# Where a pair's transposes, a batch part's values and the first FFN units stand: one reordering of an attention and gated-FFN kernel

## The chip, the cores and the metric

One NeuronCore of a Trainium2 chip. The metric is the device time of one execution in microseconds (us), the median of three runs. The kernel takes float32 inputs, computes in bfloat16 with float32 accumulation, and writes float32.

## The reference

```python
scores = q @ k.transpose(0, 1, 3, 2) / sqrt(64)      # 8 batches, 12 heads, 448 x 448
attn   = maximum(scores, 0) ** 2 / 448
x      = attn @ v                                    # heads side by side: 3584 tokens x 768
gate   = maximum(x @ w_gate, 0)                      # 768 -> 1536
out    = (gate * (x @ w_val)) @ w_out                # 1536 -> 768
```

There is no softmax: a score is cut at zero and squared. All constant factors are taken together into one scale, applied to the output.

## The kernel before, in words

The whole kernel is unrolled Python. Every instruction is pinned, so on each engine the instructions stand in the order in which the Python code emits them, and each engine works through its own list in that order. Waits come from semaphores alone.

Batches are counted from zero here. Batch 0 runs in `first_batch`, batches 1 to 7 in `batch(b)`. The FFN of batch b is cut into units (`ffn_units`) that are put between the attention work of batch b + 1, so that TensorE (PE) always has matmuls. There are two kinds of units.

- `gv_unit`: twelve matmuls of 448 columns into `g_ps`, ScalarE's relu into `g_sb`, twelve into `v_ps`, VectorE's product of both into `hT`. There are 12 such units for each batch. PE takes 2.27 us for one.
- `out_unit`: 24 matmuls of 384 columns into `o_ps`, ScalarE's scaled copy into `o_sb`, and, after the second of a tile's two units, two stores of 192 KB from SyncE's queue. There are 6 such units after an even batch, 8 after an odd one.

`mm2` issues each matmul as two halves of 64 output columns, which run side by side.

The attention of a batch works on six pairs of heads, `hp` 0 to 5, which make three parts, `qd` 0 to 2. A part has seven score tiles (`QUAD`: three for each of its two pairs and one `last` with the last 64 keys of both) and one values tile (`av`). `batch(b)` takes these 24 tiles in eight bursts of three. For each score tile, PE makes four matmuls on 64 x 64 quarters of its array, ScalarE does a relu from PSUM (`r_sb`, L166), VectorE squares it into `attn` (L170). The third tile of a burst is put into `late`, and its relu comes after the relu of the next FFN unit. For the values tile, `av_last` goes with the burst, and `av_rest` (12 matmuls) later; then VectorE copies the part's result into `xT` (L401).

A pair needs its k and q transposed. For batches 0 to 2, `transposes` does this on PE: 16 small transposes into `kq_ps` (L159), and a VectorE copy into `kq_sb` (L161). From batch 3 on (`PE_B`), DMA transposes do it, and `transpose_pair` emits nothing for PE. `PAIR_AT` says after which burst which pair's transposes come; the pair is used in the next burst or the one after it.

The score tiles, the values tiles of batches 1 to 7 and `kq_ps` share three PSUM buffers (tag `sc`) in turn; the FFN accumulators and the values banks of batch 0 share two (tag `acc`). A tile that takes a buffer waits until the tile before it in that buffer has been read.

How many units stand between two bursts is set by `gaps`: each burst n has `(before, after)` slots, before and after its `av_rest`. `gap()` takes the next share of the units that were there at the batch's start. Before, batch 1 has `[(1, 1), (1, 0)] * 4`, twelve slots, and the others sixteen. Batch 0's first six units run between batch 0 and batch 1, with the transposes of batch 1's pair 0 between the fifth and the sixth.

`low_values(b)` (L108) is a VectorE copy of some 64 rows of v within SBUF; it reads the first of the two pieces in which v is loaded. `batch(1)` does it at its start; for later batches `batch(b)` does it for b + 1 after burst 5, behind the values copy.

All loads go through GpSimd's DMA queue in program order: k, q and v of batch 0, the weights in pieces with k, q and v of batch 1 between them, `w_out` in two halves (kf 0 to 5 and 6 to 11), then k, q and v of batch 2, and so on.

In `first_batch` there are no FFN units yet; `idle_matmuls` on zeros keep PE at work. The values of part qd come with burst n as `av_at` says, and VectorE copies the two banks into `xT` (L369).

The functions that the diff touches, with the lines of the profile:

Of the kernel before, what the change touches and what calls it, by code (L numbers as in the profile page):

```python
# [11 lines left out]
AF = mybir.ActivationFunctionType  # L12
# [4 lines left out]
def kernel(  # L17
# [15 lines left out]
    nc = tc.nc  # L33
# [7 lines left out]
    NQ = HP // 2  # L41
    KD = d_model // 128
    KF = d_ff // 128
# [16 lines left out]
    def pin(ins):  # L60
        return tc.keep_in_program_order(ins)

    def mm(o, l, r, start, stop):
        pin(nc.tensor.matmul(o, lhsT=l, rhs=r, start=start, stop=stop, skip_group_check=True))  # L64

    def mm2(o, l, r, start, stop):

        for c in range(2):
            p = slice(c * 64, c * 64 + 64)
            mm(o[p], l[:, p], r, start, stop)  # L70
# [71 lines left out]
    def operands(b, hp):  # L142

        if b >= PE_B:
            n = b % NB
            return kT_b[n][:, hp, 0:S], qT_b[n][:, hp, 0:S]
        kq = transposes(b, hp)
        return kq[:, 0:S], kq[:, 512:512 + S]
# [15 lines left out]
    def relu_part(src, n):  # L164
        r = rpool.tile([128, 2, S], BF16, name="r_sb")[:, :n, :]
        pin(nc.scalar.activation(r, src, AF.Relu))  # L166
        return r
# [25 lines left out]
    def av_last(b, qd, attn, banks):  # L193

        for c, p in HALVES:
            for h2, o in HALVES:
                mm(banks[c][o, :], v_b[b % NB][p, 4 * qd + 2 * c + h2, 3, :], attn[p, 6 + h2, :], True, False)
# [7 lines left out]
    def av_bank():  # L205
        return psum.tile([128, 512], FP32, name="xT_ps", tag="acc", bufs=2)[:, :S]

    def idle_matmuls(ps, n):

        for _ in range(n):  # L210
            mm2(ps, blank[:, 0:128], blank, True, True)


    late, late_squares = [], []

    def flush_relu():
        while late:
            src, dst, n = late.pop(0)
            late_squares.append((dst, relu_part(src, n)))

    def flush():
        flush_relu()
        while late_squares:
            square_part(*late_squares.pop(0))

    def gv_unit(b, mf, xT, hT):
        c = max(i for i, (f0, _) in enumerate(CHUNKS) if f0 <= mf * 128)
        f = mf * 128 - CHUNKS[c][0]
        col = (b % 2) * S
        g_ps = psum.tile([128, 512], FP32, name="g_ps", tag="acc", bufs=2)[:, :S]  # L230
        for kd in range(KD):
            mm2(g_ps, wg_sb[c][:, kd, f:f + 128], xT[:, kd, :], kd == 0, kd == KD - 1)
        g_sb = gpool.tile([128, S], BF16, name="g_sb")
        pin(nc.scalar.activation(g_sb, g_ps, AF.Relu))  # L234
        flush_relu()
        v_ps = psum.tile([128, 512], FP32, name="v_ps", tag="acc", bufs=2)[:, :S]
        for kd in range(KD):
            mm2(v_ps, wv_sb[c][:, kd, f:f + 128], xT[:, kd, :], kd == 0, kd == KD - 1)
        pin(nc.vector.tensor_tensor(hT[:, mf, col:col + S], v_ps, g_sb, ALU.mult))  # L239
        flush()  # L240

    def segment_rows(b0, s):

        b, s = b0 + s // 7, s % 7
        r = out[b * S:(b + 1) * S, :]
        i, half = divmod(s, 2)
        if half:
            return r[256:448, :].rearrange("(j i) m -> i j m", i=3)[i]
        return r[0:256, :].rearrange("(j i) m -> i j m", i=4)[i]

    def out_unit(b0, t, c0, c1, hT, state):

        if c0 == 0:
            state[t] = opool.tile([128, d_model], FP32, name="o_sb")
        o_sb = state[t]
        o_ps = psum.tile([128, 512], FP32, name="o_ps", tag="acc", bufs=2)[:, :c1 - c0]
        for kf in range(KF):
            mm2(o_ps, hT[:, kf, bass.ts(t, 128)], wo_sb[kf // 6][:, kf % 6, c0:c1], kf == 0, kf == KF - 1)
        flush()
        pin(nc.scalar.activation(out=o_sb[:, c0:c1], in_=o_ps, func=AF.Copy, scale=float(out_scale)))  # L260
        pieces = b0 == B - 2 and t == 6
        if pieces or c1 == d_model:
            m = slice(c0 if pieces else 0, c1)
            for s in range(2):
                e = nc.sync
                if pieces and c0 > 0:
                    e = nc.gpsimd if c1 < d_model else (nc.sync, nc.scalar)[s]
                pin(e.dma_start(out=segment_rows(b0, 2 * t + s)[:, m], in_=o_sb[s * 64:s * 64 + 64, m]))  # L268

    hT_of, xT_of, o_state = {}, {}, {}  # L270
# [20 lines left out]
    def gap():  # L291

        n, of, i = share
        for _ in range((i + 1) * n // of - i * n // of):
            ffn.pop(0)()
        flush()
        share[2] = i + 1
# [22 lines left out]
    def transpose_pair(b, hp):  # L320
        kqs[b, hp] = operands(b, hp)
# [6 lines left out]
    def burst(b, tiles):  # L328

        todo, begun = [], None  # L330
        for qd, kind, c, i in tiles:
            attn = attn_of(b, qd)
            if kind == "pair":
                todo.append(scores(kqs[b, 2 * qd + c], i, attn, 8 * c + 2 * i))
            elif kind == "last":
                todo.append(scores_last((kqs[b, 2 * qd], kqs[b, 2 * qd + 1]), attn))
            else:
                ps = sc_tile()
                banks = [ps[:, c, :S] for c in range(2)]
                av_last(b, qd, attn, banks)  # L340
                begun = (qd, banks, ps[:, :, :S])
        return todo, begun

    def first_batch():
        banks = [av_bank(), av_bank()]
        idle_matmuls(banks[0], 14)
        transpose_pair(0, 0)
        idle_matmuls(banks[0], 4)
        av_at = {3: 0, 5: 1, 6: 2}
        for n in range(len(tiles_first) // 3):  # L350
            todo, _ = burst(0, tiles_first[3 * n:3 * n + 3])
            if n in av_at:
                av_last(0, av_at[n], attn_of(0, av_at[n]), banks)
            relu2(*todo[0])
            if n not in av_at:
                idle_matmuls(banks[0], 2)
            if n + 1 < HP:
                transpose_pair(0, n + 1)
            if n not in av_at:
                idle_matmuls(banks[0], 1)  # L360
            relu2(*todo[1])
            relu2(*todo[2])
            if n == 2:
                low_values(0)
            if n in av_at:
                qd = av_at[n]
                av_rest(0, qd, attn_of(0, qd), banks)
                for c in range(2):
                    pin(nc.vector.tensor_copy(xT_of[0][:, 2 * qd + c, :], banks[c]))  # L369
                banks = [av_bank(), av_bank()] if qd + 1 < NQ else None  # L370


# [3 lines left out]
    def batch(b):  # L376
        if b == 1:
            low_values(1)
        gaps = [(1, 1), (1, 0)] * 4 if b == 1 else [(1, 1)] * 8
        start_gaps(sum(map(sum, gaps)))  # L380
        pending = None
        for n in range(len(tiles_later) // 3):
            todo, begun = burst(b, tiles_later[3 * n:3 * n + 3])
            relu2(*todo[0])
            relu2(*todo[1])
            late.extend(todo[2:])
            if n == 0 and b < B - 1:
                load_qk(b + 1)
                load_v(b + 1)
            for _ in range(gaps[n][0]):  # L390
                gap()
            if n in PAIR_AT:
                hp = PAIR_AT[n]
                if hp < HP:
                    transpose_pair(b, hp)
                elif b + 1 < B:
                    transpose_pair(b + 1, 0)
            if begun:
                qd, banks, both = begun
                av_rest(b, qd, attn_of(b, qd), banks)  # L400
                pin(nc.vector.tensor_copy(xT_of[b][:, 2 * qd:2 * qd + 2, :], both))  # L401
            if b + 1 < B and n == 2 and b + 1 >= PE_B:
                dma_transposes(b + 1)
            if b + 1 < B and n == 5:
                low_values(b + 1)
            for _ in range(gaps[n][1]):
                gap()

    for b in range(B):
        xT_of[b] = xpool.tile([128, KD, S], BF16, name="xT")  # L410
        if b == 0:
            first_batch()
        else:
            batch(b)
        if b + 1 < B:
            ffn.extend(ffn_units(b))
            if b == 0:
                for _ in range(5):
                    ffn.pop(0)()
                transpose_pair(1, 0)  # L420
                ffn.pop(0)()
    flush()
    while ffn:
# [32 lines left out]
```

## Time and profile before

| what | value |
|---|---|
| median of 3 runs | 441.82 us (441.22 to 441.96) |
| profiled execution, its own time | 441.97 us |
| span of its instructions | 440.2 us |
| PE busy | 426.3 us (97%), 5076 matmuls |
| VectorE (DVE), ScalarE (ACT) busy | 210.7 us, 217.4 us |
| granted TensorE clock | 1.000 |
| DMA | 42.22 MB, mean 96 GB/s |

All times on the timeline count from the first instruction of the profiled execution. Busy time of PE counts overlapping matmuls once, so a PE that starts matmuls at an even pitch has no idle time, and a wait shows as idle time with the name of what ended it. An entry `E L12 <- F L34: a, b, c` of the waits says that engine E, at its line 12, idled a us in b places, at longest c, until something of line 34 on F ended. The time of the profiled execution is 1.8 us over its span; that part lies around the instructions.

The first matmul of the FFN (`g_ps`) starts at 29.43 us, the first score burst of batch 1 at 44.25, the first output unit at 67.01, the first FFN unit that stands in batch 2 at 86.88.

### The profile page before, as it was taken

The numbers are of one execution on the slowest core, as the hardware profiler recorded it, in microseconds if no ns is written. First come the engines' busy times: TensorE is split into PE (matmuls) and PEld (weight loads), VectorE is DVE, ScalarE is ACT, GpSimd is POOL, SyncE is SP. The second block draws the span as 40 slices with busy tenths as digits, with TensorE's granted clock in tenths as the row PEclk, the third lists the DMA queues.
The fourth block names the chain that finished last, engine by engine and source line by source line (L and its number), as shares of the span: only waits on it lengthen the run. The fifth ranks groups of instructions, "written<-read, shape, count | busy, mean of one in ns | idle before, by whom it ended". The sixth has DMA issues, their size and how long they took to land.

```text
span 440.2 us, 11446 instructions
## 1 busy us (share of the span) xinstructions
PE 426.3 (97%) x5076; PEld 251.1 (57%) x5076; DVE 210.7 (48%) x333; ACT 217.4 (49%) x322; POOL 51.9 (12%) x75
## 2 busy tenths in 40 slices
PE   7889998999999999999999999999999999999996
PEld 3447555565566555655556555655556555566664
DVE  3972655556542565445543474435653455422210
ACT  3852645545454645564635655545455545532221
POOL 8623402100024000030002100010000000000001
PEclk9999999999999999999999999999999999999999
DMA  9999999941489942194614934170322200030014
GB/s 106 179 204 195 203 205 171 192 61 28 100 104 177 180 66 64 45 191 64 118 32 96 198 67 82 37 135 2 72 56 73 73 2 1 2 94 16 1 37 108
DMA packets 80081, 42.22 MB, mean 96 GB/s; under 512 B 48640, under 2 KB 76544, under 8 KB 80032
## 3 DMA queue, kind: packets, MB, share of 16 engines
q0 software_dynamic: 47232, 23.70, 41.3%
q1 hardware_dynamic: 32720, 17.75, 16.7%
q8 instruction: 39, 0.64, 0.6%
q14 instruction: 10, 0.08, 0.1%
q10 hardware_dynamic: 80, 0.05, 0.0%
HBM read 47.19 MB, written 11.01 MB: 132 GB/s over the span
## 4 chain that ended last, share of the span: by engine, by line
PE 88%; DMA 7%; POOL 2%; DVE 1%; issue 0%; POOLq 0%; ACT 0%; DVEq 0%
PE o_ps L64 25%; PE g_ps L64 24%; PE v_ps L64 24%; PE sc_ps L64 14%; DMA qn<-in_q_dram 4%; DMA wv<-in_moe_w_val_dram 3%; PE kq_ps L159 1%; POOL kn L90 1%; POOL qn L90 1%; DVE xT L401 1%; POOL vn L90 0%; DVE kq_sb L161 0%; DVE attn L170 0%; DVE hT L239 0%; POOL wg L90 0%
## 5 line engine op out<-in xcount | busy, mean ns | idle before, releaser
L166 ACT ACTIVATE r_sb<-sc_ps 128x896 bf16<-128x896 f32 x168 | 145.4, 920 | 44.3 <-PE sc_ps L64 44.2
L170 DVE TENSOR_TENSOR attn<-r_sb 128x896 bf16<-128x896 bf16 x168 | 104.0, 623 | 91.9 <-ACT r_sb L166 91.9
L64 PE MATMUL g_ps<-xT,wg 128*64 128x448 bf16 x1152 | 126.0, 354 | 0.2 <-DVE xT L369 0.2
L64 PE MATMUL v_ps<-xT,wv 128*64 128x448 bf16 x1152 | 125.1, 352 | 0.0
L64 PE MATMUL o_ps<-wo,hT 128*64 128x384 bf16 (+1 forms) x1368 | 115.2, 324 | 0.0
L239 DVE TENSOR_TENSOR hT<-v_ps,g_sb 128x448 bf16<-128x448 f32 x96 | 59.9, 624 | 95.4 <-PE v_ps L64 95.4
L234 ACT ACTIVATE g_sb<-g_ps 128x448 bf16<-128x448 f32 x96 | 52.3, 545 | 94.1 <-PE g_ps L64 94.1
L64 PEld LDWEIGHTS <-hT 128*64 128x64 bf16 x1368 | 75.2, 110 | 37.8 <-issue 6.5
L64 PEld LDWEIGHTS <-wg 128*64 128x64 bf16 x1152 | 62.7, 110 | 49.6 <-issue 13.4
L64 PEld LDWEIGHTS <-wv 128*64 128x64 bf16 x1152 | 66.5, 110 | 42.6 <-issue 0.3
L260 ACT ACTIVATE o_sb<-o_ps 128x384 f32<-128x384 f32 (+1 forms) x57 | 27.8, 488 | 80.2 <-PE o_ps L64 80.2
L64 PE MATMUL sc_ps<-attn,vn 128*64 128x448 bf16 (+1 forms) x336 | 35.0, 354 | 0.0
L90 POOL DMA_DIRECT2D vn<-in_v_dram x16 | 12.1, 770 | 161.4 <-PE sc_ps L64 156.4
L401 DVE CAST xT<-sc_ps 128x896 bf16<-128x896 f32 x21 | 22.9, 1092 | 15.1 <-PE sc_ps L64 15.1
L64 PE MATMUL sc_ps<-qT,kT 64*64 64x448 bf16 x420 | 28.4, 357 | 0.0
L64 PEld LDWEIGHTS <-vn 128*64 128x64 bf16 (+1 forms) x384 | 19.0, 109 | 16.1 <-issue 4.9
L64 PE MATMUL sc_ps<-kq_sb 64*64 64x448 bf16 x252 | 18.3, 359 | 4.8 <-DVE kq_sb L161 2.1
L90 POOL DMA_DIRECT2D kn<-in_k_dram x20 | 14.6, 745 | 62.6 <-PE kq_ps L159 56.9
L268 POOL DMA_DIRECT2D out_dram<-o_sb x2 | 1.1, 554 | 146.2 <-ACT o_sb L260 146.2
L64 PEld LDWEIGHTS <-kT 64*64 64x64 bf16 x420 | 9.6, 105 | 14.3 <-issue 11.7
L90 POOL DMA_DIRECT2D qn<-in_q_dram x20 | 14.5, 753 | 4.9 <-DMA wv<-in_moe_w_val_dram 2.3
L161 DVE COPY kq_sb<-kq_ps 128x960 bf16<-128x960 bf16 x18 | 11.8, 654 | 6.8 <-PE kq_ps L159 6.5
(25 smaller groups left out, 80.8 us busy)
## 6 DMA issues: line engine op xcount, KB each, us to landing
out_dram<-o_sb SPq DMA_DIRECT2D x54, 192.0 KB, 2.7
vn<-in_v_dram POOLq DMA_DIRECT2D x8, 384.0 KB, 6.1
kn<-in_k_dram POOLq DMA_DIRECT2D x7, 384.0 KB, 9.2
qn<-in_q_dram POOLq DMA_DIRECT2D x7, 384.0 KB, 11.8
vn<-in_v_dram POOLq DMA_DIRECT2D x8, 288.0 KB, 6.9
wo<-in_moe_w_out_dram POOLq DMA_DIRECT2D x2, 1152.0 KB, 20.4
kn<-in_k_dram POOLq DMA_DIRECT2D x7, 288.0 KB, 10.2
qn<-in_q_dram POOLq DMA_DIRECT2D x7, 288.0 KB, 12.6
```

Source lines behind the costliest of these rows:

```text
L64: pin(nc.tensor.matmul(o, lhsT=l, rhs=r, start=start, stop=stop, skip_group_check=True))
L90: pin(nc.gpsimd.dma_start(out=o, in_=i))
L159: pin(nc.tensor.transpose(o, t[:, 2 * hp + h2, i, :], ident))
L161: pin(nc.vector.tensor_copy(kq, ps[:, 0:512 + S]))
L166: pin(nc.scalar.activation(r, src, AF.Relu))
L170: pin(nc.vector.tensor_tensor(dst, r, r, ALU.mult))
L234: pin(nc.scalar.activation(g_sb, g_ps, AF.Relu))
L239: pin(nc.vector.tensor_tensor(hT[:, mf, col:col + S], v_ps, g_sb, ALU.mult))
L260: pin(nc.scalar.activation(out=o_sb[:, c0:c1], in_=o_ps, func=AF.Copy, scale=float(out_scale)))
L268: pin(e.dma_start(out=segment_rows(b0, 2 * t + s)[:, m], in_=o_sb[s * 64:s * 64 + 64, m]))
L401: pin(nc.vector.tensor_copy(xT_of[b][:, 2 * qd:2 * qd + 2, :], both))
```

## The change

The transposes of a pair are not emitted where they are due, but put into a list, `midway`, which the next FFN unit empties in its middle: between the `g_ps` and the `v_ps` matmuls of a `gv_unit`, or after half of the matmuls of an `out_unit`. They are put into the list before the burst's first slots, so they go with the next unit, whichever slot holds it.

In batch 1 the slots are now `(0, 1), (1, 1), (1, 1), (0, 1), (0, 1), (0, 1), (0, 1), (1, 1)`, eleven in all; each burst has a unit behind its `av_rest`. In batch 2, burst 5 has both its units behind `av_rest`. The other batches keep their slots.

Seven units of batch 0, not six, run before batch 1, and the transposes of batch 1's pair 0 stand in the middle of the seventh.

In batch 0, the first part's values come with burst 4, not 3, and its `low_values` after burst 3, not 2. The first bank of the last part is copied into `xT` by ScalarE.

```diff
+    def run_midway():
+        while midway:
+            midway.pop(0)()
...
         pin(nc.scalar.activation(g_sb, g_ps, AF.Relu))
         flush_relu()
+        run_midway()
         v_ps = psum.tile([128, 512], FP32, name="v_ps", tag="acc", bufs=2)[:, :S]
...
         for kf in range(KF):
+            if kf == KF // 2:
+                run_midway()
             mm2(o_ps, hT[:, kf, bass.ts(t, 128)], wo_sb[kf // 6][:, kf % 6, c0:c1], kf == 0, kf == KF - 1)
...
-        av_at = {3: 0, 5: 1, 6: 2}
+        av_at = {4: 0, 5: 1, 6: 2}
...
-            if n == 2:
+            if n == 3:
                 low_values(0)
...
-                    pin(nc.vector.tensor_copy(xT_of[0][:, 2 * qd + c, :], banks[c]))
+                    x = xT_of[0][:, 2 * qd + c, :]
+                    if (qd, c) == (NQ - 1, 0):
+                        pin(nc.scalar.activation(x, banks[c], AF.Copy))
+                    else:
+                        pin(nc.vector.tensor_copy(x, banks[c]))
...
-        gaps = [(1, 1), (1, 0)] * 4 if b == 1 else [(1, 1)] * 8
+        gaps = [(1, 1)] * 8
+        if b == 1:
+            gaps = [(0, 1), (1, 1), (1, 1), (0, 1), (0, 1), (0, 1), (0, 1), (1, 1)]
+        elif b == 2:
+            gaps[5] = (0, 2)
...
-            for _ in range(gaps[n][0]):
-                gap()
             if n in PAIR_AT:
                 hp = PAIR_AT[n]
                 if hp < HP:
-                    transpose_pair(b, hp)
+                    midway.append(lambda hp=hp: transpose_pair(b, hp))
                 elif b + 1 < B:
-                    transpose_pair(b + 1, 0)
+                    midway.append(lambda: transpose_pair(b + 1, 0))
+            for _ in range(gaps[n][0]):
+                gap()
...
-                for _ in range(5):
+                for _ in range(6):
                     ffn.pop(0)()
-                transpose_pair(1, 0)
+                midway.append(lambda: transpose_pair(1, 0))
                 ffn.pop(0)()
```

More of the change, by code (lines that the diff above doesn't have):

```diff
@@ L211, in idle_matmuls @@
             mm2(ps, blank[:, 0:128], blank, True, True)
-    late, late_squares = [], []
+    late, late_squares, midway = [], [], []
+    def run_midway():
+        while midway:
+            midway.pop(0)()
     def flush_relu():
```

## The prediction

> **What bounds the kernel now.** I read in this order: busy shares, busy time by stretch, PE's waits, PE's timeline around each wait, and the loads that the moved work needs. PE is busy 426.3 of 440.2 us. By stretch (busy us of PE, PEld, DVE, ACT, POOL with counts, then granted clock, DMA share, GB/s):
>
> ```profile
> 44.20:86.90 42.70, 39.45 (x532) 23.26 (x530) 24.71 (x40) 24.90 (x35) 8.47 (x12) 1.00 1.26 192
> 86.90:141.80 54.90, 54.90 (x696) 32.87 (x692) 28.18 (x44) 26.44 (x41) 7.45 (x11) 1.00 0.56 95
> 141.80:388.00 246.20, 246.19 (x2846) 141.56 (x2844) 123.79 (x191) 131.98 (x196) 10.79 (x15) 1.00 0.44 76
> ```
>
> From 86.9 to 388 us PE never idles and nothing can be saved there. PE loses time only in the first batch, at the first transposes of batch one (counted from zero) and in batch one, 44 to 87 us. PE's waits in that last stretch (total, times, longest):
>
> ```profile
> PE sc_ps L64 <- DVE kq_sb L161: 1.9, 2, 0.9
> PE sc_ps L64 <- DVE xT L401: 1.4, 2, 0.7
> ```
>
> PE's timeline at the five places (start, length, what, count, idle before and releaser):
>
> ```profile
> 40.78 0.42 PE L159 MATMUL kq_ps<-ident,kn 128*64 128x128 bf16 x8
> 41.64 0.41 PE L159 MATMUL kq_ps<-ident,qn 128*64 128x128 bf16 x8 [0.44 <-DMA qn<-in_q_dram]
> ...
> 53.79 0.36 PE L64 MATMUL sc_ps<-attn,vn 64*64 64x448 bf16 x4
> 55.09 0.38 PE L64 MATMUL sc_ps<-kq_sb 64*64 64x448 bf16 x4 [0.94 <-DVE kq_sb L161]
> ...
> 65.18 0.57 PE L64 MATMUL sc_ps<-kq_sb 64*64 64x448 bf16 x8
> 66.69 0.38 PE L64 MATMUL sc_ps<-kq_sb 64*64 64x448 bf16 x4 [0.94 <-DVE kq_sb L161]
> ...
> 75.37 0.57 PE L64 MATMUL sc_ps<-kq_sb 64*64 64x448 bf16 x8
> 76.63 0.38 PE L64 MATMUL sc_ps<-kq_sb 64*64 64x448 bf16 x4 [0.69 <-DVE xT L401]
> ...
> 85.31 0.57 PE L64 MATMUL sc_ps<-kq_sb 64*64 64x448 bf16 x8
> 86.56 0.38 PE L64 MATMUL sc_ps<-kq_sb 64*64 64x448 bf16 x4 [0.68 <-DVE xT L401]
> ```
>
> Matmuls overlap, so I count start to start. A score tile of four takes 0.21 us (53.58 to 53.79), a half transpose 0.22. Lost are therefore 41.64-41.00 = 0.64, 55.09-54.00 = 1.09, 66.69-65.60 = 1.09, 76.63-75.79 = 0.84 and 86.56-85.73 = 0.83: together **4.49 us**. Two are a kq copy with too little work between transposes and burst, two a values copy (1.09 us on DVE) whose bank the next burst's third tile needs.
>
> The loads land one after another at about 192 GB/s until 75 us. The two that matter, with issue and, from the DMA issues, KB and us to landing:
>
> ```profile
> 41.79 0.82 POOL L90 DMA_DIRECT2D wo<-in_moe_w_out_dram  x1 [0.71 <-DMA qn<-in_q_dram]
> 51.56 0.74 POOL L90 DMA_DIRECT2D vn<-in_v_dram  x1 [1.46 <-DMA wg<-in_moe_w_gate_dram]
> ```
> ```profile
> wo<-in_moe_w_out_dram POOLq DMA_DIRECT2D x1, 1152.0 KB, 22.5
> ```
> ```profile
> vn<-in_v_dram POOLq DMA_DIRECT2D x1, 384.0 KB, 21.7
> ```
>
> So the second half of w_out lands at 64.3, and the first piece of batch two's v at 73.3. In the kernel before nobody waits for either: the first output matmul starts at 67.01, and DVE copies the low values (which need that piece) late:
>
> ```profile
> 75.48 1.09 DVE L401 CAST xT<-sc_ps 128x896 bf16<-128x896 f32 x1 [0.48 <-PE sc_ps L64]
> 76.61 0.28 DVE L108 COPY vn<-vn 64x384 bf16<-64x384 bf16 x1
> ```
>
> **The change, part by part.** The work is the same: no matmul is added or removed. The order of PE's instructions is the old one again from late in batch two on.
>
> Transposes inside a unit. Sixteen cost 0.44 us wherever they stand (40.78 aside: 47.24 to 47.69), and before and after them the pitch of the FFN matmuls does not change (47.24 follows 46.10 by 12 x 0.0946). Cost nothing. Twelve pairs move; three of them now interrupt an accumulation (output units), of which no row exists: 0 to 0.25 each (a change to score tiles and back costs 0.1 + 0.02 to 0.15), I take 0, the nearest row being the one between units. The kq copy (0.66) now has half a unit behind it, 1.14 us of v_ps or 0.98 of o_ps; that removes the two 1.09 waits. If the cover goes, each returns.
>
> A unit behind each part's values. The L401 copy lies under a unit of at least 1.95 us: the 0.84 and 0.83 go.
>
> Seven units ahead. The first transposes of batch one come at 29.43 + 6 x 2.27 + 1.14 = 44.2, after qn's landing near 41.5: the 0.64 goes.
>
> First batch. The values of the first part no longer wait for vn (0.38 at 17.57), and ACT's 1.55 us without work before 20.56 shrinks. But two batch parts, not one, now want their banks right after a copy; the wait there was 0.81 + 0.15. ACT's copy of the last bank's first half (0.54, as g_sb of the same size) runs beside DVE's and lets g_ps start about 0.3 earlier. Between 1 us earlier and 1 later; I take 0.2 earlier. The next step says why it hardly matters.
>
> New waits. From g_ps at 29.43: seven units 15.89, transposes 0.44, burst 0.81, unit 2.29 + 0.44, burst 0.81, units 2.29 + 0.44 + 2.27, burst 0.81, unit 2.29 + 0.44, values 1.14, unit 2.27, burst 0.81. The first output unit starts at 62.9, four us before its old time. Half of it (0.98) and the transposes (0.44) bring PE to 64.3, when w_out's second half lands: a wait of 0 to 0.6. Then 0.98 of the unit, burst 0.78, unit 1.97, burst 0.75, values 1.14: PE is at 70.0, and DVE, behind the squares of that burst (ACT's relus end at 70.5), does the values copy from 71.05 to 72.14. Next in its queue stands the low-values copy of batch two, which waits for v at 73.3; behind it now stands pair five's kq copy, which before stood ahead of it. DVE idles 1.2 us; everything up to here is thus free by 1.2 us either way. Then 0.05 + 0.31 + 0.66 + 0.05: the second tile of that burst starts at **74.36** instead of 75.59, PE having waited some 1.65 us. ACT, SP and POOL hold no one up: in the segments with one unit ACT needs 3 x 0.81 + 0.49 = 2.9 us, PE takes 2.75 to 3.2.
>
> From that tile on the remaining work of batch one is the same, three output units and a burst, less the 0.84 and 0.83 waits. Sum: 75.59 - 74.36 + 0.84 + 0.83 = **2.90 us**. So 1.6 of the 4.49 come back as a wait for v.
>
> One price is left: the first output tile's two stores (384 KB) go out at 68.9 instead of 71.66 (output unit two ends at 68.0, ACT's copy at 68.85), 4.4 us ahead of v's landing. Rows: stores issued at 79.64 found loads under way, and the qn piece due 3.2 us later landed 0.9 late, the one due 4.8 us later 2.2 late; at 127.33, kn due in 2.8 us was 0.3 late, qn due in 5 us 2.1 late; at 71.66, v due in 3.2 us was on time. Ends 0 and 2.1. v's bytes are mostly through well before it lands, which brings it near the earlier rows; I take 0.4. By the Trainium skill, DMA: Bandwidth & Descriptors, Queues, rings and completion order, each DMA engine alternates between the queues that have work, packet by packet; the stores would then put v back by their full share, an estimate of 2.0 us, and the sum would be 440.9. The row against it: the stores of 79.64 moved no byte before 83 us.
>
> The profiled execution took 441.97 with span 440.2, 0.15 over the median 441.82. 441.97 - 2.90 + 0.4 = 439.47; against the median **439.3**.
>
> **Rivals.** *Stores push v back* by 1 to 2.1 us: gain 0.8 to 1.9, 439.9 to 441.0; for it the late rows, against it the one on time. There the Trainium skill speaks against the change once more (TensorE: Matmul & The Clock Gate, What's actually happening: an idle window of about 3.4 us halves the clock): a wait of 1.65 + 2.1 could cross it and cost an estimate of 1.7 us more; no row here shows a granted clock below 1.00, but no wait was that long.
>
> *v is not last*: if it lands before 72.1, the whole of the 1.2 us comes too: gain 4.1, 437.7. For it only that loads may run 2% quicker elsewhere.
>
> *Slower*: low values wait for the whole of v, whose second piece lands 1.55 later (74.86), and that is 2.2 late behind the stores. The copy starts at 77.1, 3.75 later: 2.90 - 3.75, so 442.7. It decides from a copy at 76.2 on. Against it: the copy at 17.55 ran before the second piece's landing (18.82), and the instruction waits for one load alone.
>
> *It brings nothing*: each moved pair costs 0.25 where it now stands, 12 x 0.25 = 3.0, which eats the gain: 442.3; the rows between units speak against it.
>
> **How the numbers follow.** My forecast 0.62 (438.6 to 439.9), stores 0.20, v not last 0.10, slower 0.04, nothing 0.04. A measurement of this kernel tells about 0.2%, 0.9 us, from no change. Faster: 0.62 + 0.10 + 0.15 of the stores' 0.20 = 0.87; same 0.08; slower 0.05. The range runs from 438.3 (v 1 us early) to 441.0 (v 2.1 late): outside are most of v not last, slower and nothing.
>
> **What would show it.** Right: no wait for L401, none at the first transposes, none of a kq copy but one, of 1.5 us or more near 72 to 74 us, while DVE waits for vn, with its vn copy starting at v's landing; w_out waited for under 0.6 us; PE without a gap from there to 388 us. Wrong: the vn copy at once when DVE reaches it (then more is gained), or later than 74.5 (less); waits of PE after 75 us; transposes longer than 0.44.

## The result and the profile after

The changed kernel takes 439.0 us in the median of four runs (438.73 to 439.12), the kernel before on the same chip 441.73: a ratio of 0.9939, with a 95% interval of 0.9922 to 0.9956. That is 2.7 us faster, and the forecast was 439.3, a gain of 2.5. The profiled execution took 438.88 us with a span of 437.0, where that of before took 441.97 with 440.2: 3.1 us, since these two executions lie 0.12 below and 0.24 above their medians.

The busy time by stretch (start and end, length, then busy us of PE, PEld, DVE, ACT and POOL with counts, granted clock, DMA share, GB/s), cut at the places that match those of before:

```profile
44.00:84.00 40.00, 38.99 (x542) 23.02 (x538) 24.44 (x40) 23.86 (x34) 8.20 (x11) 1.00 1.33 201
84.00:139.00 55.00, 55.00 (x696) 32.92 (x692) 28.30 (x44) 27.37 (x42) 7.49 (x10) 1.00 0.54 96
139.00:385.00 246.00, 245.98 (x2842) 141.54 (x2840) 124.04 (x191) 131.54 (x196) 10.46 (x14) 1.00 0.44 77
```

The stretch of batch one has 1.01 us of idle PE left, where before 3.25 of 42.70 us were idle. PE's waits from 44 to 390 us are one line (total, times, longest):

```profile
PE sc_ps L64 <- DVE kq_sb L161: 1.0, 1, 1.0
```

Both entries of before in this stretch, two waits for a kq copy and two for L401, are gone; the one that stands here is new. PE's timeline (start, length, what, count, idle time before and releaser) at the first moved transposes, in the first output unit, and at the new wait:

```profile
44.22 0.42 PE L159 MATMUL kq_ps<-ident,kn 128*64 128x128 bf16 x8
...
62.88 1.17 PE L64 MATMUL o_ps<-wo,hT 128*64 128x384 bf16 x12
63.88 0.39 PE L159 MATMUL kq_ps<-ident,kn 128*64 128x128 bf16 x8
64.10 0.39 PE L159 MATMUL kq_ps<-ident,qn 128*64 128x128 bf16 x8
64.33 1.14 PE L64 MATMUL o_ps<-wo,hT 128*64 128x384 bf16 x12
...
72.50 0.56 PE L64 MATMUL sc_ps<-kq_sb 64*64 64x448 bf16 x5
74.08 0.57 PE L64 MATMUL sc_ps<-kq_sb 64*64 64x448 bf16 x7 [1.01 <-DVE kq_sb L161]
```

An output unit that is interrupted by the transposes still takes its 1.00 us for the first half, and 0.45 go to the transposes. The burst at 72.50 shows the price that is left: its first tile of four takes 0.21, so the second could start at 72.71 and starts at 74.08, 1.37 us later. The fifth matmul of the first line is issued and then stands, which is why the idle figure says 1.01 only. VectorE's timeline says why:

```profile
71.08 1.08 DVE L416 CAST xT<-sc_ps 128x896 bf16<-128x896 f32 x1
73.05 0.28 DVE L108 COPY vn<-vn 64x384 bf16<-64x384 bf16 x1 [0.88 <-DMA vn<-in_v_dram]
73.36 0.66 DVE L161 COPY kq_sb<-kq_ps 128x960 bf16<-128x960 bf16 x1
```

The values copy ends at 72.16, the copy of batch two's low values waits for the load of v, and the kq copy that PE needs is queued behind it. GpSimd's timeline and the DMA issues (KB each, us from issue to landing) give the landing of both pieces of v:

```profile
51.29 0.74 POOL L90 DMA_DIRECT2D vn<-in_v_dram  x1 [2.18 <-DVE attn L170]
53.01 0.74 POOL L90 DMA_DIRECT2D vn<-in_v_dram  x1 [0.97 <-DMA wv<-in_moe_w_val_dram]
```
```profile
vn<-in_v_dram POOLq DMA_DIRECT2D x1, 384.0 KB, 21.7
...
vn<-in_v_dram POOLq DMA_DIRECT2D x1, 288.0 KB, 22.6
```

The first lands at 73.0, the second at 75.6. The first matmul of the FFN starts at 29.47 (before 29.43), the first FFN unit that stands in batch two at 83.63 (before 86.88), and the spans differ by 3.2: the whole gain lies between these two places.

### The profile page after: what moved, and what is told of

It reads as the page before. It is cut to its first block, busy times and chain, and to the rows that moved or that the text cites. A ratio compares the mean times of both kernels' runs of the same rounds, so it can differ in the third digit from the quotient of the medians.

```text
span 437.0 us, 11447 instructions
## 1 busy us (share of the span) xinstructions
PE 425.9 (97%) x5076; PEld 251.2 (57%) x5076; DVE 210.3 (48%) x332; ACT 217.3 (50%) x323; POOL 51.9 (12%) x75
## 4 chain that ended last, share of the span: by engine, by line
PE 88%; DMA 6%; DVE 3%; ACT 2%; issue 1%; POOL 1%; POOLq 0%; DVEq 0%; ACTq 0%
PE g_ps L64 25%; PE v_ps L64 24%; PE o_ps L64 24%; PE sc_ps L64 13%; DMA vn<-in_v_dram 5%; PE kq_ps L159 1%; ACT r_sb L166 1%; DVE attn L170 1%; DMA qn<-in_q_dram 1%; DVE kq_sb L161 1%; PE xT_ps L64 0%; POOL kn L90 0%; DVE xT L380 0%; DVE hT L244 0%; POOL qn L90 0%
## 5 line engine op out<-in xcount | busy, mean ns | idle before, releaser
L64 PEld LDWEIGHTS <-wv 128*64 128x64 bf16 x1152 | 66.3, 110 | 41.2 <-issue 0.3
```

## The experiments

The theory: the value lies in the moved transposes; the other edits only exchange waits, and what is left is the wait for v through VectorE's queue. The rivals are that the first batch's part brings something, that a unit less ahead of batch one would do as well, that the wait is one for the load itself, whatever VectorE's order, and that transposes inside an accumulation cost something. The moved transposes alone have no run with `PE_B = 3`, and a late copy of the low values has none on the changed kernel as it stands: the first was measured with all pairs on PE, the second with two other orders of the first batch. Each ratio is against the kernel before on the same chip, as a median with its 95% interval.

### Six units ahead of batch one instead of seven

```diff
             if b == 0:
-                for _ in range(6):
+                for _ in range(5):
                     ffn.pop(0)()
```

> The changed kernel with six units of batch zero ahead of batch one, not seven; batch one's last slot then holds two units. Load-stream theory: v lands when it lands, so a unit less before that point only lengthens the wait there (1.4 to about 3.6 us), and one output unit more (2.0 us) stands behind it: 439.0 + 2.0 = 441.0. Rival (no anchor; the work is the same and the first transposes find qn landed): 439.0, at most 439.6.

Measured: 442.29 us in the median of twelve runs, ratio 1.0002 (0.9984 to 1.002). The twelve make two groups: five from 440.40 to 440.76 and seven from 442.09 to 443.92. The profiled execution, 443.56, is of the upper group. Its windows, from just before the wait:

```profile
70.70:74.40 3.70, 0.62 (x11) 0.15 (x9) 1.01 (x3) 1.30 (x2) 2.20 (x3) 1.00 1.46 178
74.40:76.00 1.60, 1.60 (x13) 0.67 (x15) 0.68 (x2) 1.17 (x2) 0.00 (x0) 0.57 1.37 213
76.00:77.50 1.50, 1.50 (x18) 1.02 (x16) 0.41 (x1) 0.56 (x1) 0.00 (x0) 0.50 1.34 279
77.50:78.50 1.00, 1.00 (x20) 0.84 (x18) 0.38 (x1) 0.00 (x0) 0.00 (x0) 0.74 1.49 210
78.50:80.00 1.50, 1.50 (x24) 0.67 (x22) 0.81 (x2) 0.87 (x2) 0.00 (x0) 1.00 1.46 200
```
```profile
70.74 0.56 PE L64 MATMUL sc_ps<-kq_sb 64*64 64x448 bf16 x5
74.39 0.78 PE L64 MATMUL sc_ps<-kq_sb 64*64 64x448 bf16 x7 [3.08 <-DVE kq_sb L161]
...
75.09 2.13 PE L64 MATMUL o_ps<-wo,hT 128*64 128x384 bf16 x12
```

One unit less ahead brings PE to the burst earlier, and the load does not come earlier: the second tile could start at 70.95 and starts 3.4 us later, at 74.39, no earlier than the changed kernel's 74.08, with one unit more (2.0) still to do. The lower group is 1.4 to 1.8 us over the changed kernel's 439.0, or 1.2 to 1.6 with each taken against before on its own chip. The trace would give 0.3 + 2.0 = 2.3 without the clock, and there is no trace of that group to say where the rest went. The upper group has something on top. The granted clock (third column from the end) falls to 0.57 and 0.50 after the wait, and half an output unit behind a burst takes 2.13 us where it takes 1.17 in the changed kernel. Worked out from the windows, 1.6 x 0.43 + 1.5 x 0.50 + 1.0 x 0.26 = 1.7 us are lost by it. Another microsecond of this execution's excess lies outside its instructions: its time is 2.8 us over its span of 440.8, where the profiled executions of before and after are 1.8 and 1.9 over theirs. The clock is shown for this one execution. Whether the six others of the group had the same is not shown: their mean clocks over the span, 0.992 to 0.996, overlap with the lower group's, 0.995 to 0.999. So the seventh unit is worth some 1.4 us, and in the traced execution the wait without it was long enough for the clock to fall.

### The first batch as it was

```diff
-        av_at = {4: 0, 5: 1, 6: 2}
+        av_at = {3: 0, 5: 1, 6: 2}
...
-            if n == 3:
+            if n == 2:
                 low_values(0)
...
-                    x = xT_of[0][:, 2 * qd + c, :]
-                    if (qd, c) == (NQ - 1, 0):
-                        pin(nc.scalar.activation(x, banks[c], AF.Copy))
-                    else:
-                        pin(nc.vector.tensor_copy(x, banks[c]))
+                    pin(nc.vector.tensor_copy(xT_of[0][:, 2 * qd + c, :], banks[c]))
```

> The changed kernel with the first batch of the kernel before (first values with burst 3, low values after burst 2, all copies on VectorE). Load-stream theory: the first FFN matmul may move by 0.2 to 0.3 us either way, and the wait for v takes it up: 439.0 within 0.2. Rival (the new order of the first batch is a part of the gain): slower by 0.3 to 1.0, 439.3 to 440.0.

Measured: 438.83 us, ratio 0.9948 (0.9934 to 0.9962), which cannot be told from the changed kernel's 0.9939. The FFN starts at 29.11, 0.36 us earlier than with the new first batch. At the wait:

```profile
73.61 0.57 PE L64 MATMUL sc_ps<-kq_sb 64*64 64x448 bf16 x7 [0.90 <-DVE kq_sb L161]
```

The edit of the first batch brings nothing: it even starts the FFN later, and the wait for v takes that up. The traces show how much later. Counted from a score burst near 14 us that all of them share (14.01 in the changed kernel, 14.19 in before), the FFN starts after 15.46 us in all five with the new first batch, after 14.98 in four of the five with the old one, and after 15.24 in that of before. So the edit costs the first batch 0.48 us against those four.

### The low values' copy behind the unit, first batch as it was

On top of the previous edit:

```diff
-            if b + 1 < B and n == 5:
-                low_values(b + 1)
             for _ in range(gaps[n][1]):
                 gap()
+            if b + 1 < B and n == 5:
+                low_values(b + 1)
```

> The same old first batch in the kernel with the late low-values copy, where nothing waits for v any more. Load-stream theory: what the first batch gains or loses now reaches the end, up to the 0.3 us by which PE came after the second half of w_out (63.99 against 64.33): 437.6 with 0.3 either way; the two first batches differ by no more than that, since the first FFN matmul started at 29.43 and 29.47. Rival (new first batch worth 0.5 or more): 438.1 or more.

Measured: 437.73 us (437.58 to 437.98), ratio 0.9912 (0.9898 to 0.9925). Against the kernel without this edit on the same chip, 438.83 (438.77 to 440.09), it is 1.1 us, and the two sets of runs do not overlap. PE waits for no kq copy any more, and is idle for the second half of w_out for 0.23 us. PE's burst and VectorE's two copies:

```profile
72.65 0.85 PE L64 MATMUL sc_ps<-kq_sb 64*64 64x448 bf16 x12
```
```profile
72.23 0.65 DVE L161 COPY kq_sb<-kq_ps 128x960 bf16<-128x960 bf16 x1
72.94 0.43 DVE L108 COPY vn<-vn 64x384 bf16<-64x384 bf16 x1
```

The first piece of v lands no earlier than without the edit (72.9 against 72.5); only VectorE's order differs. So the wait was one of order.

### The same, with the new first batch but its low values early

```diff
-            if n == 3:
+            if n == 2:
                 low_values(0)
...
-            if b + 1 < B and n == 5:
-                low_values(b + 1)
             for _ in range(gaps[n][1]):
                 gap()
+            if b + 1 < B and n == 5:
+                low_values(b + 1)
```

> The late low-values copy, and batch zero's low-values copy back after burst 2, with the first values still at burst 4. In the changed kernel PE waited 0.64 us there (19.46 to 20.10) for that copy, which stood behind a square. Load-stream theory: 0.4 to 0.6 us earlier first FFN matmul, of which w_out's landing lets 0.3 through: 437.3. Rival (ScalarE's relus set the first batch): 437.6, no change.

Measured: 437.56 us (437.51 to 438.50), ratio 0.9913 (0.9899 to 0.9926): 4.0 us faster than before, by the ratios 1.1 faster than the changed kernel, which was run on another chip, and not to be told from the run above. PE's and VectorE's timelines:

```profile
64.19 1.17 PE L64 MATMUL o_ps<-wo,hT 128*64 128x384 bf16 x12 [0.21 <-DMA wo<-in_moe_w_out_dram]
...
72.39 0.85 PE L64 MATMUL sc_ps<-kq_sb 64*64 64x448 bf16 x12
```
```profile
71.97 0.65 DVE L161 COPY kq_sb<-kq_ps 128x960 bf16<-128x960 bf16 x1
73.64 0.28 DVE L108 COPY vn<-vn 64x384 bf16<-64x384 bf16 x1 [1.02 <-DMA vn<-in_v_dram]
```

VectorE still waits a microsecond for v, but now behind the kq copy, and the burst's twelve matmuls run through. The FFN starts at 28.96, 14.73 us after the burst near 14 us. Against the new first batch's 15.46, the later low values of batch zero thus cost 0.73 us, and against the old one's 14.98 the rest of the edit saves 0.25. But the end moves by 0.2 at most against the run above, within the scatter. By then w_out's second half ends a wait again (it lands at 64.2), and a start that is earlier still would mostly wait for it; that this alone takes up the gain was not tried apart.

### Batch two's v loaded before its k and q

```diff
-                load_qk(b + 1)
-                load_v(b + 1)
+                if b == 1:
+                    load_v(b + 1)
+                    load_qk(b + 1)
+                else:
+                    load_qk(b + 1)
+                    load_v(b + 1)
```

> The changed kernel with batch two's v loaded ahead of its k and q. Load-stream theory: the low-values copy finds v landed (near 66 us) and the kq wait goes, but q's last piece now lands where v's did (74.5 to 75.6), and batch two's first transposes, reached 1.4 us earlier at 74.4, wait for it instead, 0.2 to 1.3 us: 437.8 to 438.9. Rival (the wait is not the loads'): 439.0 with the kq wait unchanged.

Measured: 438.77 us (438.45 to 439.69), ratio 0.9939 (0.9926 to 0.9951), the same as the changed kernel. The wait for the kq copy shrinks to 0.16 us of idle time, 0.5 from start to start, since v lands at 66.3 and only the low-values copy itself now stands ahead. But q is last in the queue, and its transposes come 1.0 us late:

```profile
76.13 0.41 PE L159 MATMUL kq_ps<-ident,qn 128*64 128x128 bf16 x8 [0.81 <-DMA qn<-in_q_dram]
```

The wait has moved from one load to another. Exchanging the loads brings nothing here: the stream brings the three in the same time.

### All batches' transposes on PE: before, after, and each half of the change

In these four, `PE_B = B`, so that 30 more pairs are transposed on PE and not by DMA. The 30 pairs add some 13 us to each, and the four are compared with each other. The first two are the kernels before and after with this one edit:

```diff
-    PE_B = 3
+    PE_B = B
```

> The kernel before with the transposes of all batches on TensorE (PE_B = 8); the base for the next three. Thirty more pairs at 0.44 us: 441.7 + 13.2 = 454.9. Up to 86 us the same five waits as in the kernel before (0.64, 1.09, 1.09, 0.84, 0.83). Both theories say the same here.

> The changed kernel with the transposes of all batches on TensorE: 42 pairs stand in the middle of units, not 12. Load-stream theory: transposes inside a unit cost nothing by themselves, so the gap to the same base is the gap of the change, 2.7 +- 0.3 us: 452.2. Rival (an interrupted accumulation costs 0.1 us or more): the gap shrinks by 30 times that, to nothing or below.

Measured: 454.44 us, ratio 1.0283 (1.0255 to 1.0311), for before; 452.34, ratio 1.0243 (1.0203 to 1.0283; its four runs lie between 451.48 and 454.57), for after. A pair between units costs (454.44 - 441.40) / 30 = 0.43 us, and one inside a unit, after's 452.34 against 439.0 of another chip, 0.44. The timeline of after's variant shows an output unit that is interrupted:

```profile
224.71 1.17 PE L64 MATMUL o_ps<-wo,hT 128*64 128x384 bf16 x12
225.71 0.39 PE L159 MATMUL kq_ps<-ident,kn 128*64 128x128 bf16 x8
225.93 0.39 PE L159 MATMUL kq_ps<-ident,qn 128*64 128x128 bf16 x8
226.16 1.14 PE L64 MATMUL o_ps<-wo,hT 128*64 128x384 bf16 x12
```

From 224.71 to the next work, at 227.13, it takes 2.42 us: a plain unit in the same trace takes 1.98 (238.11 to 240.09), and the transposes 0.45. Nothing is paid for the interruption, and PE has no wait from 86 us to its last batch; the wait for the kq copy, near 73 us, is 0.3 us of idle time here.

Then the moved transposes alone (first batch, slots and six units as before), and the whole change without them, with the transposes back between the two slots. Of the first edit, the part in `batch`:

```diff
+            if n in PAIR_AT:
+                hp = PAIR_AT[n]
+                if hp < HP:
+                    midway.append(lambda hp=hp: transpose_pair(b, hp))
+                elif b + 1 < B:
+                    midway.append(lambda: transpose_pair(b + 1, 0))
             for _ in range(gaps[n][0]):
                 gap()
-            if n in PAIR_AT:
-                hp = PAIR_AT[n]
-                if hp < HP:
-                    transpose_pair(b, hp)
-                elif b + 1 < B:
-                    transpose_pair(b + 1, 0)
...
```

> Of the change only the transposes in the middle of a unit, with the slots, the first batch and the six units ahead of the kernel before. Load-stream theory: the two kq waits and the wait for qn go (2.8), the two waits for the values copy (0.84, 0.83) stay, and nothing waits for v, since the kq copy stands ahead of the low-values copy: 454.9 - 2.8 = 452.1, level with the whole change. Rival (slots and seventh unit do the work): 454 or more.

> The whole change but for the transposes, which stand where they were due between the two slots. Load-stream theory: the five waits of the base go (4.5) and nothing waits for v, but behind bursts with an empty first slot the transposes wait for the relu of the burst's first tile, whose PSUM buffer they take: 0.7 to 0.9 us at five places, 3.5 to 4.5 in all, so 453.9 to 454.9, little or no gain. Rival (the place of the transposes is worth little): 450.4 to 452.2.

Measured: 452.38 us (452.00 to 452.48), ratio 1.0234 (1.0206 to 1.0262), with the moved transposes alone, which is level with the whole change, as far as its runs' scatter of 3 us allows to say; 454.88 (454.75 to 455.47), ratio 1.0297 (1.0262 to 1.0331), with all but them, which is no faster than before. PE's waits after 44 us, of the first and then of the second:

```profile
PE sc_ps L64 <- DVE xT L408: 1.4, 2, 0.7
```
```profile
PE kq_ps L159 <- ACT r_sb L166: 3.6, 5, 0.8
```

With the moved transposes alone the two kq waits are gone and the two behind the values copies stay (L408 is L401 of before). With everything else alone the values copies are covered, but five transposes now come straight behind a burst, and wait for the relu of the burst's first score tile, whose PSUM buffer they take: 0.64 to 0.83 us each. The first of the five:

```profile
46.14 0.76 PE L64 MATMUL sc_ps<-kq_sb 64*64 64x448 bf16 x12
47.54 0.41 PE L159 MATMUL kq_ps<-ident,kn 128*64 128x128 bf16 x8 [0.64 <-ACT r_sb L166]
```

The move into the unit's middle is thus also what makes the new slots possible.

## Why the prediction was right, step by step

- **Transposes inside a unit, 0 with an end of 0.25.** 0: the half units before and after keep 1.00 and 1.07 us, and the variant with all pairs on PE repeats it. Four of the twelve pairs interrupt an output unit, not three; the fourth does so at 119.99. The rival "brings nothing" had its whole price here.
- **The waits that go, 4.49 us.** All five went. The moved transposes alone remove the two of kq (the one of qn is only 0.14 in the variant of before with all pairs on PE): 454.44 - 452.38 = 2.06 us, for twice 1.09.
- **The first FFN matmul, 0.2 earlier.** It is 0.04 later on the timeline and 0.22 later from the burst near 14 us on (15.46 against 15.24): the wrong sign. What the prediction left out is PE's wait at 20.10 for the low values, which now stand behind burst 3 (0.47 us idle); with them back behind burst 2 it is 14.73, 0.5 earlier than in before. As the prediction said, it hardly matters, since the wait for v comes behind it.
- **w_out's second half, a wait of 0 to 0.6.** 0 (PE at 64.33, forecast 64.3; the half was issued at 40.83 and landed 23.2 us later, at 64.0). With half a microsecond taken out ahead it is 0.2.
- **The wait for v, the second tile at 74.36.** The chain was right to the order of the three copies: values copy to 72.16 (forecast 72.14), low values at v's landing, kq copy, tile. The tile starts at 74.08, because v landed at 73.0 and not 73.3. Such a difference is scatter: the landing of this piece lies between 72.5 and 73.6 in the ten traces that load v last. That it came so close to the forecast is in part luck. PE's wait is 1.37 us, a little under the 1.5 that the prediction named as its sign.
- **The stores, 0.4 of 0 to 2.1.** This term was mis-sized. They were issued at 68.84, as forecast (68.9). The first piece of v came 1.9 us behind the load ahead of it (71.06, from an issue at 48.36 and 22.7 us), as in before, so the stores cost it 0. The second piece came 2.6 us behind the first instead of 1.6, so a delay of about 1 us fell on that one, for which nobody waits. The traces point to the stores as its cause: in the seven with the first stores at 68.5 to 69.4 the last piece came 2.1 to 2.6 us behind the one ahead of it, in the four with the stores at 70.5 to 71.7 it came 1.6 behind; no run was made with the stores alone moved. The DMA queues of the changed kernel show how: the stores, issued at 68.84 and 69.46, moved no byte before 71 us, and 0.34 of their 0.39 MB from 72 to 74, when the loads moved 0.15 MB in the two microseconds instead of the 0.19 or so of each microsecond before. The Trainium skill (DMA: Bandwidth & Descriptors, Queues, rings and completion order) says that a DMA engine takes turns, packet by packet, between the queues that have work. The sharing from 72 to 74 us agrees with it; the estimate made from it, with the stores' full share put on the first piece, 2.0 us late and 440.9 in all, did not come true.

Together: 75.59 - 74.08 + 0.84 + 0.83 = 3.18 us were gained, where 2.90 - 0.4 = 2.5 had been forecast; the 0.28 of v's landing and the 0.4 of the stores are the difference. 441.97 - 3.18 = 438.79 beside the profiled 438.88. By the medians the gain is 2.7, nearer to the forecast; the rest of the 3.18 is the scatter of the two profiled executions.

The rivals: *v is not last* did not come, but the runs with the late copy show what it is worth, 1.1 us, at 437.6 to 437.7, where the rival had put 437.7. *Slower* would have needed a copy that waits for the second piece; it started at 73.05, 2.6 us before that piece landed. Within *Stores push v back* stood the clock: the changed kernel's 1.4 us of standing left the granted clock at 1.00 from 74 us on, and the traced execution of the kernel with six units ahead, where PE stood for some 3.4 us, shows it at 0.57 and 0.50 for a stretch, with a loss of 1.7 us. That agrees with the Trainium skill (TensorE: Matmul & The Clock Gate, What's actually happening), by which an idle window of about 3.4 us halves the clock, and with the 1.7 us that were estimated from it.

## What to carry to other kernels

Short work of an engine whose result another engine must still copy is best put into the middle of a long unit of the same engine: the second half covers the copy, and here the interruption was free. Before work is pulled forward, look up when each load lands that it or its neighbours need, and in each in-order queue put the instruction that waits for a load behind the ones that others wait for: here one line moved was worth 1.1 us of what the earlier reordering had left. When a reordering removes several waits, add up what the next wait gives back; 1.4 of 4.5 us came back here, and with a single unit less ahead the wait was 3.4 and the gain over before was nothing in the median of twelve runs.

## What the runs showed of the hardware

- A wait of PE of some 3.4 us was followed by a granted clock of 0.50 to 0.57 for about three microseconds, in the profiled execution of the kernel with six units ahead; 384-column matmuls then took 2.13 us for twelve instead of 1.17. Five of the kernel's twelve executions were 1.3 to 3.5 us quicker than the others; how long PE waited in them, and with what clock, is not shown.
- Stores of 384 KB issued from 68.84 us on, behind a loaded queue, moved no byte before 71 us. The load due 4.2 us after the issue kept its pace, and the one behind it came about 1 us late, while the loads' rate fell to less than half from 72 to 74 us.
